# Attention into a gated MLP on one Trainium2 core: the tokens of the first two batches on 96 partitions, and new orders for all engines

## The chip, the cores and the metric

The kernel runs on one core of a Trainium2 chip. The metric is device time in microseconds (us). The core has a matrix engine (TensorE, PE in the profile; its weight loads stand as PEld), a vector engine (VectorE, DVE), an activation engine (ScalarE, ACT), a general engine (GpSimd, POOL) and a queue processor that issues most transfers (SyncE, SP). Transfers run on 16 DMA engines. SBUF is the on-chip memory with 128 partitions, PSUM the accumulator that TensorE writes.

## The reference

There are 8 batches, 8 heads, 576 tokens per head and batch, 64 numbers per token and head, and 32 "pack" queries per head. First the pack queries attend to the tokens, then the tokens attend to the 32 packed results, and the concatenated heads (512 numbers per token, 4608 tokens) go through a two-layer MLP whose activation is h times sigmoid(beta h):

```python
def sm_attn(qq, kk, vv):
    s = scale * np.matmul(qq, kk.transpose(0, 1, 3, 2))
    s = s - np.max(s, axis=-1, keepdims=True)
    a = np.exp(s)
    a = a / (np.sum(a, axis=-1, keepdims=True) + 1e-09)
    return np.matmul(a, vv)
p_packed = sm_attn(p, k, v)
out = sm_attn(q, p_packed, p_packed)
...
h = x @ w_in                                  # 512 -> 2048
g = h * (1.0 / (1.0 + np.exp(-beta * h)))
return (g @ w_out).astype(np.float32)         # 2048 -> 512
```

## The kernel before, in words

**Work of one batch.** k, q and v are loaded in float32 and cast to bfloat16 (`cast`). k and q are transposed, so that the 64 numbers of a head lie on partitions: for batches 0 and 1 on TensorE (`tr`) with copies out of PSUM (`T`), from batch 2 on by transposing DMAs on SP. `s1`, `e1`, `z1`, `i1`, `pun`, `pp` are the first attention (scores, exponentials, sums, inverses, packed values, their copy). `s2`, `e2`, `z2`, `l2`, `n2`, `A2` are the second one, whose normalised weights are `A2`. The packed values are multiplied with w_in ahead of time (`w`, scaled on DVE into `W`), so the first MLP layer is `h` = W times A2, 16 blocks of 128 rows for 512 tokens; ACT applies the activation (`g`). The second layer is `o` (batches 0 and 1, 32 products each, and the leftover tokens) or `p`/`P`, a form with seven products in place of eight (batches 2 to 7).

**Tokens 512 to 575, the rests.** A batch of 576 tokens is cut into 512 main tokens, four on each of 128 partitions, and 64 rest tokens. For k, q and v each rest is loaded by two DMAs of 64 partitions (four heads to partitions 0 to 63, four to 64 to 127; tiles `kr`, `qr`, `vr`), cast on its own, transposed on its own (`trr`), copied on its own (`rk`, `rq`) and has its own scores (`s1r`) and exponentials (`e1r`). In the MLP the rests of two batches share `hr`, `gr` and the product `o` with t = 4, whose two halves are stored by two DMAs (`o_rest`).

**Order.** Nothing schedules at run time. `SEQUENCE` is a table with one list of tasks for each engine, and each engine runs its list in order. `Planner.run` walks through the five lists with a cost in microseconds for each task; with the lists fixed, the costs decide only how the instruction streams are written out and how many keep-warm matmuls (`o_ps<-identr`, result unused) are put into TensorE's gaps before 60 us. SP's list is one queue: a load that waits for its staging buffer holds back all that stand behind it.

**Staging.** w_in and w_out come in four pieces of 1 MB each through three buffers (`stage`). In float32 k, q and v have one buffer of 128 x 2048 each; batches 0 and 1 fill it with two DMAs of 512 KB (four heads each), the later ones with one of 1 MB. Half the first layer of batch 0 can be computed when w_in pieces 0 and 1 are there; its second layer needs all four pieces of w_out, and is cut in two (`HALVED`): `o` 1 to 7 need pieces 0 and 1, `o` 9 to 15 pieces 2 and 3.

**Lines.** All matmuls stand at L382 and all transposes on TensorE at L387, so groups are told apart by tiles. Loads of k, q, v: L434, of rests: L442; of w_in and w_out: L1245 and L1255; casts: L463 (main), L473 (rests), L1251 and L1262 (weights); copies of transposes: L520 and L540; exponentials: L585 and L605; `W`: L795; `A2`: L736; `g`: L827; copy and store of the leftover tokens: L892 and L906.

Of the kernel before, what the change touches and what calls it, by code (L numbers as in the profile page):

```python
# [8 lines left out]
B, H, S, D = 8, 8, 576, 64  # L9
# [12 lines left out]
NC = 4  # L22
# [21 lines left out]
HALVED = (0,)  # L44
TILED = {"w": 1, "s2": 1}
TILED_US = 0.095
# [9 lines left out]
        ("brow", 0), ("tr", 0, "k", 0), ("tr", 0, "k", 1), ("p0_tr", 0), ("p0_tr", 1), ("bcol",), ("brow", 1),  # L56
        ("trr", 0, "k"), ("s1r", 0), ("tr", 0, "q", 0), ("brow", 2), ("s1", 0, 1), ("s1", 0, 0), ("tr", 0, "q", 1),
        ("z1", 0), ("pun", 0, 0), ("pun", 0), ("brow", 3), ("s2", 0, 0), ("z2", 0, 0), ("z2", 0, 1), ("w", 0, 0),
        ("w", 0, 1), ("h", 0, 1), ("h", 0, 2), ("tr", 1, "k", 0), ("h", 0, 0), ("h", 0, 3), ("tr", 1, "k", 1),
        ("o", 0, 0, 1), ("o", 0, 1, 1), ("h", 0, 7), ("h", 0, 4), ("o", 0, 1, 3), ("w", 0, 2), ("trr", 1, "k"),  # L60
        ("o", 0, 0, 3), ("h", 0, 5), ("h", 0, 8), ("s1r", 1), ("trr", 0, "q"), ("h", 0, 6), ("o", 0, 1, 5),
        ("s1", 1, 0), ("o", 0, 0, 5), ("o", 0, 0, 7), ("h", 0, 11), ("s1", 1, 1), ("h", 0, 9), ("o", 0, 1, 7),
        ("o", 0, 2, 1), ("w", 0, 3), ("o", 0, 2, 3), ("o", 0, 3, 1), ("o", 0, 3, 3), ("o", 0, 2, 5), ("z1", 1),
        ("o", 0, 3, 5), ("h", 0, 14), ("o", 0, 2, 7), ("h", 0, 15), ("tr", 1, "q", 0), ("h", 0, 13), ("pun", 1, 0),
        ("h", 0, 12), ("pun", 1), ("tr", 1, "q", 1), ("h", 0, 10), ("o", 0, 3, 7), ("s2", 0, 1), ("s2", 1, 0),
        ("o", 0, 1, 9), ("o", 0, 0, 9), ("w", 1, 0), ("o", 0, 0, 11), ("o", 0, 1, 11), ("z2", 1, 0), ("o", 0, 1, 13),
        ("trr", 1, "q"), ("o", 0, 1, 15), ("z2", 1, 1), ("z2", 0, 2), ("o", 0, 0, 13), ("o", 0, 0, 15),
        ("o", 0, 3, 9), ("o", 0, 3, 11), ("s2", 1, 1), ("w", 1, 1), ("o", 0, 2, 9), ("o", 0, 3, 13), ("z2", 1, 2),
        ("o", 0, 2, 11), ("w", 1, 2), ("o", 0, 2, 13), ("h", 1, 2), ("o", 0, 2, 15), ("h", 1, 1), ("o", 0, 3, 15),
        ("h", 1, 0), ("w", 1, 3), ("h", 1, 5), ("h", 1, 3), ("p_tr", 1), ("h", 1, 4), ("o", 1, 0, 1), ("h", 1, 11),  # L70
        ("p_tr", 0), ("h", 1, 6), ("o", 1, 0, 3), ("h", 1, 8), ("o", 1, 1, 1), ("h", 1, 9), ("h", 1, 10),
        ("o", 1, 1, 3), ("hr", 0, 0), ("h", 1, 7), ("o", 1, 0, 5), ("o", 1, 1, 5), ("s1r", 2), ("hr", 0, 1),
        ("s1", 2, 1), ("o", 1, 0, 7), ("s1", 2, 0), ("h", 1, 15), ("o", 1, 0, 9), ("o", 1, 0, 11), ("o", 1, 1, 7),
        ("z1", 2), ("pun", 2, 0), ("o", 1, 1, 9), ("pun", 2), ("o", 1, 1, 11), ("h", 1, 13), ("h", 1, 12),
        ("w", 2, 0), ("w", 2, 1), ("h", 1, 14), ("o", 1, 1, 13), ("hr", 1, 0), ("o", 1, 0, 13), ("o", 1, 0, 15),
        ("hr", 1, 1), ("o", 1, 1, 15), ("s2", 2, 0), ("w", 2, 2), ("o", 1, 2, 1), ("o", 1, 2, 3), ("z2", 2, 0),
# [274 lines left out]
class Kernel:  # L351
# [57 lines left out]
    def task(self, key, engine, us, fn, deps=(), rank=0, **kw):  # L409
# [4 lines left out]
        return t  # L414


    def plan_loads(self, b):
        nc = self.nc
        rank = 100 * b
        early = b < PE_BATCHES  # L420
        for xi, x in enumerate("kqv" if b == 0 else "kvq"):
            src = self.src[x]
            last = [] if b == 0 else [("cast", b - 1, x, i) for i in range(2)]
            lastr = [] if b == 0 else [("cast", b - 1, x, 2)]
# [919 lines left out]
```

## Time and profile before

| what | us |
|---|---|
| median of 3 runs (246.19 to 246.64) | 246.43 |
| the profiled execution's own time | 246.91 |
| its span, first to last instruction | 245.1 |
| TensorE busy | 231.1 |
| VectorE busy | 148.7 |
| ScalarE busy | 178.8 |
| GpSimd busy | 58.8 |

The profiled execution took 1.8 us more than its span, and 0.5 us more than the median. A busy TensorE includes keep-warm matmuls (132 of them), and waits between dependent matmuls. A row of a stage gives its bounds, then length, the busy time of PE, PEld, DVE, ACT and POOL with the number of instructions, the granted clock of TensorE (1.00 is full), the share of the 16 DMA engines' time that was busy (over 1 when packets overlap), and the rate in GB/s. A row of the timeline gives start, length, engine, line, operation, tiles and shapes, and in brackets the idle time before it and what ended it.

### The profile page before, as it was taken

Reading aid. Unit: us, or ns where it says so; the run is one execution under the profiler, and the core shown is the slowest. Engines: PE = TensorE matmul, PEld = TensorE weight load, DVE = VectorE, ACT = ScalarE, POOL = GpSimd, SP = SyncE. Lnnn points to the kernel's source line nnn. Section 1 sums busy time; section 2 is a strip of 40 time slices with the busy share of each in tenths; the row PEclk is TensorE's granted clock in tenths of the full one; section 3 lists DMA queues with packets and bytes.
Section 4 is the critical chain, followed back from the end, with each engine's and each line's share of the span. In section 5 each row is a group of like instructions: output and inputs, shape, how many; then the busy total and the mean of one; then the engine's idle time right before and its main releaser. Section 6 shows DMA issues by size and latency. Waiting matters only on the chain.

```text
span 245.1 us, 5810 instructions
## 1 busy us (share of the span) xinstructions
PE 231.1 (94%) x2429; PEld 151.0 (62%) x2429; DVE 148.7 (61%) x239; ACT 178.8 (73%) x317; POOL 58.8 (24%) x75
## 2 busy tenths in 40 slices
PE   3997779989999999999999999999999999999992
PEld 3985434633464444787578744886587557667870
DVE  6455566676907937872788376843993368813521
ACT  2486959887797897797779767988798769766210
POOL 4002313206443034207430541061305000000000
PEclk9999999999999999999999999999999999999999
DMA  6999999999989999999999999995993141004024
GB/s 195 298 332 376 305 356 312 366 256 292 199 270 143 277 301 344 183 292 285 280 176 304 325 276 187 337 228 133 195 289 75 36 171 45 1 0 174 0 77 140
DMA packets 74826, 54.13 MB, mean 221 GB/s; under 512 B 42688, under 2 KB 68304, under 8 KB 74800
## 3 DMA queue, kind: packets, MB, share of 16 engines
q1 hardware_dynamic: 74496, 53.68, 85.0%
q8 instruction: 19, 0.31, 0.5%
q10 hardware_dynamic: 304, 0.07, 0.2%
q14 instruction: 7, 0.06, 0.1%
HBM read 37.23 MB, written 9.44 MB: 190 GB/s over the span
## 4 chain that ended last, share of the span: by engine, by line
PE 73%; DMA 16%; issue 5%; POOL 3%; SPq 1%; DVE 0%; POOLq 0%
PE o_ps L382 42%; PE h_ps L382 19%; DMA kr<-in_k_dram 6%; DMA k<-in_k_dram 5%; DMA v<-in_v_dram 5%; PE hr_ps L382 3%; PE w_ps L382 3%; PE s_ps L382 2%; PE z_ps L382 2%; PE pp_ps L382 1%; POOL k_bf L463 1%; POOL p_dup L1172 1%; POOL w_in_bf L1251 1%; SPq L434 0%; PE pT_ps L387 0%
## 5 line engine op out<-in xcount | busy, mean ns | idle before, releaser
L827 ACT ACTIVATE g_main<-h_ps 128x512 bf16<-128x512 f32 x128 | 71.6, 595 | 29.7 <-PE h_ps L382 29.5
L382 PEld LDWEIGHTS <-g_main 128*128 128x128 bf16 x608 | 57.0, 98 | 27.0 <-issue 4.0
L382 PE MATMUL o_ps<-w_out_bf,g_main 128*128 128x256 bf16 (+1 forms) x416 | 72.2, 306 | 0.9 <-ACT w_out_bf L1262 0.5
L382 PE MATMUL h_ps<-A2T,W_bf 128*128 128x512 bf16 x256 | 69.8, 380 | 0.9 <-DVE A2T L736 0.6
L795 DVE SCALAR_TENSOR_TENSOR W_bf<-w_ps,rz,beta_bc 128x512 bf16<-128x512 f32 x64 | 45.1, 745 | 14.5 <-PE w_ps L382 14.4
L382 PEld LDWEIGHTS <-W_bf 128*128 128x128 bf16 x512 | 32.2, 98 | 22.7 <-issue 5.5
L397 ACT ACT_TABLE_LOAD x24 | 30.8, 1283 | 1.1 <-PEq L1328 0.7
L1043 DVE TENSOR_TENSOR o_sb<-o_ps,o_sb 128x512 f32<-128x512 f32 x18 | 12.4, 690 | 24.2 <-PE o_ps L382 21.5
L382 PE MATMUL o_ps<-w_sum,g_main 128*128 128x256 bf16 x192 | 25.9, 273 | 0.0
L382 PE MATMUL o_ps<-w_sum,g_sum 128*128 128x256 bf16 x192 | 24.8, 273 | 0.0
L463 POOL CAST v_bf<-v 128x1024 bf16<-128x1024 f32 x14 | 15.0, 1082 | 37.9 <-DMA v<-in_v_dram 29.0
L382 PEld LDWEIGHTS <-g_sum 128*128 128x128 bf16 x192 | 18.1, 98 | 4.1 <-issue 0.5
L463 POOL CAST q_bf<-q 128x1024 bf16<-128x1024 f32 x12 | 13.2, 1116 | 28.2 <-DMA q<-in_q_dram 14.9
L463 POOL CAST k_bf<-k 128x1024 bf16<-128x1024 f32 x14 | 15.2, 1101 | 16.7 <-DMA k<-in_k_dram 9.7
L382 PE MATMUL o_ps<-w_out_bf,g_rem 128*128 128x512 bf16 x64 | 16.3, 380 | 0.0
L382 PE MATMUL o_ps<-identr 128*128 128x128 bf16 x132 | 11.7, 244 | 3.7 <-DVE bones L1108 3.7
L1045 ACT COPY o_sb<-o_ps 128x512 f32<-128x512 f32 x12 | 7.0, 587 | 10.0 <-PE o_ps L382 10.0
L382 PE MATMUL w_ps<-w_in_bf,pp 64*32 64x512 bf16 x256 | 11.9, 383 | 2.3 <-POOL w_in_bf L1251 1.3
L382 PEld LDWEIGHTS <-identr 128*128 128x128 bf16 x132 | 9.5, 111 | 5.7 <-DVE bones L1108 3.7
L382 PEld LDWEIGHTS <-pp 64*32 64x32 bf16 x384 | 4.3, 89 | 13.5 <-issue 9.3
L695 ACT ACTIVATE E2T<-s_ps,rz 128x512 bf16<-128x512 f32 x16 | 10.7, 688 | 1.8 <-PE s_ps L382 1.3
L736 DVE TENSOR_TENSOR A2T<-E2T,rz 128x512 bf16<-128x512 bf16 x16 | 11.1, 691 | 1.4 <-ACT rz L731 1.4
(99 smaller groups left out, 261.1 us busy)
## 6 DMA issues: line engine op xcount, KB each, us to landing
out_dram<-o_sb SPq DMA_DIRECT2D x14, 512.0 KB, 3.6
k<-in_k_dram SPq DMA_DIRECT2D x6, 1024.0 KB, 8.9
q<-in_q_dram SPq DMA_DIRECT2D x6, 1024.0 KB, 9.1
v<-in_v_dram SPq DMA_DIRECT2D x6, 1024.0 KB, 8.1
w_in<-in_moe_w_in_dram SPq DMA_DIRECT2D x4, 1024.0 KB, 10.3
w_out<-in_moe_w_out_dram SPq DMA_DIRECT2D x4, 1024.0 KB, 10.5
k<-in_k_dram SPq DMA_DIRECT2D x4, 512.0 KB, 9.8
q<-in_q_dram SPq DMA_DIRECT2D x4, 512.0 KB, 7.6
```

What stands on the lines that cost most here:

```text
L382: return self.nc.tensor.matmul(out, lhsT, rhs, start=start, stop=stop, tile_position=pos, skip_group_check=True)
L397: self.nc.scalar.preload_act_table_set(SETS[mode])
L463: self.copy[engine](o[:, 0:2048].rearrange("p (t h d) -> p h t d", t=4, h=8)[:, h], t[:, 0:2048].rearrange("p (h t d) -> p h t d", h=8, t= ...
L695: nc.scalar.activation(st[b, "E2"][:, i, 0:SM], st[b, "s2", i][:], AF.Exp, scale=st[b, "rz1"][:, 2 + i : 3 + i])
L736: nc.vector.tensor_tensor(part(st[b, "A2"], i), part(st[b, "E2"], i), st[b, "rz2"][:, i] if i < 2 else st[b, "rz2r"][:], ALU.mult)
L795: nc.vector.scalar_tensor_tensor(st[b, "W"][:, r, cols], st[b, "w", m][:], st[b, "rz1"][:, r : r + 1], self.beta_bc[:, cols], op0=ALU.mult ...
L827: nc.scalar.activation(st[b, "g"][:, ft, :], st[b, "h", ft][:], AF.Silu)
L1043: nc.vector.tensor_tensor(o, x, o, ALU.add)
L1045: self.copy[engine](o, x)
L1172: self.copy[engine](self.p_dup[0:LATER, :, e, :], self.p32[0:LATER])
L1251: self.copy[engine](self.w_in_bf[:, c, 512 * n : 512 * n + 512], self.t["w_in", n][:, c])
```

## The change

1. **96 partitions.** Batches 0 and 1 put all 576 tokens of a head as six consecutive tokens on each of 96 partitions (`TP, TT = 96, 6`). k, q and v come in two DMAs each of four heads (96 partitions x 4 x 1536 bytes, 576 KB). No rest DMAs, rest casts, rest transposes, `s1r` or `e1r` are left in these batches. Casts are half as long again (1536 numbers on each partition), transposes come in four groups of six for k and for q (one for each pair of heads) with a copy of 576 numbers each, the first attention's scores in three parts in place of two and a rest, its sums in six steps in place of five.
2. **Staging.** The float32 halves go to shared places: the three old buffers and a tile `X` in one of the two buffers of `g`. The second bfloat16 halves of k, q and a part of v go to a tile `Y` in one of the two buffers of `W`. So `w` of batch 1 now waits for the last transposes of batch 1, and `h` of batch 1 for its casts. A batch-1 half waits for the cast of the half before it in its place (`FIRST_SLOTS`).
3. **Zeros.** The fifth block of `E1T` is cleared by POOL after its use in batches 0 and 1 (`ez`), not at the start.
4. **The last product.** In batch 7 the leftover tokens' `o` is computed in two halves of 256 columns (t = 4 and t = 5), each with its own copy and two stores, one on SP's queue and one on ACT's.
5. **Lists.** All five lists of `SEQUENCE` are new. In batch 0 the casts of k move from DVE to ACT, the first cast of v and one of w_in from DVE to POOL. TensorE changes between its plain and its tiled form (`w`, `s2`) 66 times in place of 60, ACT its table 21 times in place of 23, and 111 keep-warm matmuls are left of 132.

```diff
+TP, TT = 96, 6
+FIRST_SLOTS = (
+    {"k": ("k32", "X0"), "q": ("q32", "X1"), "v": ("v32", "k32")},
+    {"k": ("X0", "q32"), "v": ("X1", "v32"), "q": ("k32", "X0")},
+)
...
     "PE": [
-        ("brow", 0), ("tr", 0, "k", 0), ("tr", 0, "k", 1), ("p0_tr", 0), ("p0_tr", 1), ("bcol",), ("brow", 1),
-        ("trr", 0, "k"), ("s1r", 0), ("tr", 0, "q", 0), ("brow", 2), ("s1", 0, 1), ("s1", 0, 0), ("tr", 0, "q", 1),
...
+        ("p0_tr", 0), ("brow", 0), ("bcol",), ("tr", 0, "k", 0), ("tr", 0, "k", 1), ("brow", 1), ("tr", 0, "k", 2),
+        ("tr", 0, "q", 0), ("tr", 0, "k", 3), ("tr", 0, "q", 1), ("brow", 2), ("s1", 0, 0), ("s1", 0, 1),
+        ("tr", 0, "q", 3), ("s1", 0, 2), ("p0_tr", 1), ("tr", 0, "q", 2), ("z1", 0), ("pun", 0, 0), ("pun", 0),
+        ("s2", 0, 0), ("z2", 0, 0), ("w", 0, 0), ("z2", 0, 1), ("brow", 3), ("w", 0, 1), ("h", 0, 3), ("h", 0, 1),
+        ("h", 0, 2), ("h", 0, 0), ("tr", 1, "k", 1), ("tr", 1, "k", 0), ("h", 0, 6), ("h", 0, 5), ("tr", 1, "k", 3),
...
     "SP": [
-        ("ld", 0, "k", 0), ("ld", 0, "k", 1), ("ld", "p0", 1), ("ld", 0, "k", 2), ("ld", 0, "q", 0),
-        ("ld", 0, "v", 0), ("ld", 0, "q", 1), ("ld", 0, "v", 1), ("ld", 0, "v", 2), ("ld_in", 0), ("ld_in", 1),
-        ("ld_out", 0), ("ld", 1, "k", 0), ("ld", 1, "k", 1), ("ld_in", 2), ("ld", 1, "k", 2), ("ld", 0, "q", 2),
-        ("ld_out", 1), ("ld_in", 3), ("ld", 1, "q", 0), ("ld", 1, "v", 0), ("ld", 1, "v", 1), ("ld", 1, "v", 2),
-        ("ld", 1, "q", 1), ("ld_out", 2), ("ld_out", 3), ("ld", 1, "q", 2), ("ld", 2, "k", 0), ("ld", 2, "k", 2),
+        ("ld", 0, "k", 0), ("ld", 0, "k", 1), ("ld", 0, "q", 0), ("ld", 0, "q", 1), ("ld", "p0", 1),
+        ("ld", 0, "v", 0), ("ld", 0, "v", 1), ("ld_in", 0), ("ld_in", 1), ("ld_out", 0), ("ld", 1, "k", 0),
+        ("ld", 1, "k", 1), ("ld_in", 2), ("ld_out", 1), ("ld_in", 3), ("ld", 1, "q", 0), ("ld", 1, "v", 0),
+        ("ld", 1, "q", 1), ("ld", 1, "v", 1), ("ld_out", 2), ("ld_out", 3), ("ld", 2, "k", 0), ("ld", "p"),
...
     "POOL": [
-        ("cast", 0, "k", 2), ("w_in", 0, 0), ("cast", 1, "k", 0), ("cast", 1, "k", 1), ("cast", 1, "k", 2),
+        ("p0_bf", 0), ("cast", 0, "v", 0), ("w_in", 0, 0), ("ez", 0), ("w_in", 1, 0), ("cast", 1, "k", 0),
+        ("w_in", 3, 0), ("cast", 1, "q", 0), ("cast", 1, "v", 0), ("ez", 1), ("p_dup", 0), ("cast", 2, "k", 0),
...
     "DVE": [
+        ("pT", 1), ("i1", 0), ("w_in", 0, 1), ("W", 0, 0), ("w_in", 1, 1), ("A2", 0, 0), ("A2", 0, 1), ("W", 0, 1),
...
+    def plan_first_loads(self, b):
...
+                def load(x=x, i=i, slot=slot):
+                    if slot in ("X0", "X1"):
+                        if "X" not in self.t:
+                            self.t["X"] = self.gp.tile([128, 4096], f32, tag="g", name="x32")
...
+                    nc.sync.dma_start(
+                        t[0:TP, 0:1536].rearrange("p (h e) -> p h e", h=4),
+                        self.src[x][b, 4 * i : 4 * i + 4].rearrange("h (p t) d -> p h (t d)", p=TP),
+                    )
...
+                ld = last = self.task(("ld", b, x, i), "SP", us, load, [self.slot_user.get(slot)], rank + xi)
...
+        def transpose(x, c):
+            st[b, x, "ps", c] = ps = self.att(f"{x}T_ps", bf16)
+            for t in range(TT):
+                self.tp(ps[:, TP * t : TP * t + TP], self.first_block(b, x, c, t), self.identr[0:TP, 0:TP])
...
+        if first:
+            self.task(("ez", b), "POOL", 0.35, lambda: nc.gpsimd.memset(E()[:, 4, :], 0.0), [z1, last], rank + 20)
...
+                n = slice(256 * (t - 4), 256 * (t - 3)) if halves and t >= 4 else slice(0, DM)
...
+            if halves and t >= 4:
+                nc.vector.tensor_copy(st[b, "ob", 2][:, 0, 256 * (t - 4) : 256 * (t - 3)], st[b, "o", t][:, 0:256])
...
+                    queue = nc.scalar if halves and e else nc.sync
+                    queue.dma_start(self.out[lo : lo + SR, n], o[64 * e : 64 * e + 64, 0, n])
```

## The prediction

> **What bounds the kernel now.** I read the page's 40 slices first, then a table of stages, then the timeline where the stages change. The slices (span, engine busy in tenths, DMA share, rate):
>
> ```profile
> span 245.1 us, 5810 instructions
> ...
> PE   3997779989999999999999999999999999999992
> ...
> DMA  6999999999989999999999999995993141004024
> ```
>
> TensorE has gaps only in the first nine slices (up to about 55 us) and in the last; the DMA engines are full for 27 slices. The table of stages (length, then busy time of PE, PEld, DVE, ACT, POOL; the last two numbers are DMA share and GB/s):
>
> ```profile
> 0.00:24.50 24.50, 19.16 (x260) 17.02 (x261) 13.70 (x35) 13.28 (x21) 4.91 (x11) 1.00 0.99 300
> 24.50:58.00 33.50, 29.64 (x271) 14.37 (x269) 22.90 (x41) 28.05 (x52) 8.33 (x9) 1.00 1.10 311
> 58.00:237.00 179.00, 178.59 (x1886) 118.13 (x1884) 110.91 (x163) 136.87 (x245) 45.60 (x56) 1.00 0.81 197
> ```
>
> From 58 us, where the `h` of batch 1 begin, TensorE idles 0.4 us in 179: time falls there only if TensorE gets less work, and it doesn't. Before 24.5 us it mostly waits or runs keep-warm matmuls. Between, it idles 33.5 - 29.64 = 3.9 us, and rows of `o_ps<-identr` (0.55, 0.22, 0.28 and 0.79 us) add 1.8 us of filling. So between the first `h` and those of batch 1 at most 5.7 us can go. What ends the waits there is in the timeline; each of these rows waited for a piece of w_in or w_out:
>
> ```profile
> 31.61 1.30 DVE L1251 CAST w_in_bf<-w_in 128x1024 bf16<-128x1024 f32 x2 [2.34 <-DMA w_in<-in_moe_w_in_dram]
> ...
> 35.57 0.88 DVE L1262 TENSOR_SCALAR w_out_bf<-w_out,rbeta 128x512 bf16<-128x512 f32 x2 [0.73 <-DMA w_out<-in_moe_w_out_dram]
> ```
>
> ```profile
> 51.55 1.33 ACT L1262 ACTIVATE w_out_bf<-w_out,rbeta 128x512 bf16<-128x512 f32 x2 [0.70 <-DMA w_out<-in_moe_w_out_dram]
> ```
>
> So the bound up to 58 us is the order and rate of loads. The rates, by stretches in which one kind of load runs:
>
> ```profile
> 9.00:12.00 3.00, 3.00 (x42) 2.79 (x42) 1.25 (x5) 2.53 (x4) 0.00 (x0) 1.00 1.10 349
> 16.00:20.00 4.00, 3.59 (x53) 2.64 (x49) 1.42 (x5) 2.87 (x5) 0.51 (x1) 1.00 1.05 386
> ...
> 28.00:30.00 2.00, 2.00 (x23) 1.41 (x24) 0.69 (x1) 1.63 (x5) 0.88 (x1) 1.00 1.26 216
> 30.00:32.00 2.00, 2.00 (x10) 0.75 (x8) 0.39 (x1) 1.33 (x3) 0.00 (x0) 1.00 1.09 273
> 32.00:34.00 2.00, 1.11 (x14) 0.53 (x14) 1.76 (x4) 1.13 (x3) 0.73 (x1) 1.00 1.03 361
> ...
> 53.00:57.00 4.00, 4.00 (x37) 1.68 (x34) 3.79 (x8) 3.25 (x10) 0.33 (x1) 1.00 1.08 198
> ```
>
> The first row is main loads of 1 KB pieces on 128 partitions, the second is w_in (2 KB pieces), rows three to five the rests `kr` and `qr` (256-byte pieces on 64 partitions), the last the rests of batch 2 with `p`, the only load before that lies on 96 partitions.
>
> **The change part by part.** I sum against the profiled execution: 246.91 us, 1.8 over its span; the median, 246.43, lies 0.5 lower.
>
> *Loads.* A 512 KB half takes 524 KB / 349 = 1.50 us. The two pairs of rests between 28 and 34 us cost 2 x (169 + 112 + 24) / 385 = 1.58 us of lost rate beside the weights' 385, 0.79 a pair, and 131 KB / 385 = 0.34 for their own bytes: 1.13 a pair. After, a half is 590 KB. On its price the sum hangs. Packets of 1.5 KB lie between the 1 KB and the 2 KB rows, 349 and 386, so 1.61 us at 367. No 128-partition row shows what 96 partitions do; the 96-partition row has 198 GB/s, or 2.98 us. I take 1.69 us, the 1 KB row's rate with no credit for longer pieces: 198 is a mixture with rests, and 128-partition loads beside rests fall as low (216, 273).
>
> Up to the last piece of w_out, before had 12 halves and five pairs of rests ahead: 18.0 + 5.65 = 23.65 us. After: 12 x 1.69 = 20.3, 3.4 us less. On the way: w_in 0 (batch 0 alone, two pairs) 11.26 against 10.14, 1.1 earlier; w_in 2, 0.7 earlier; w_out 1 and w_in 3, where `kr` and `qr` no longer stand ahead, 3.0 earlier, 32.6 and 35.4 us; the last w_out 48.2 in place of 51.5. The batch 2 loads come 4.5 earlier, as a sixth pair goes.
>
> A rule weighs against this. The Trainium skill's SBUF — State Buffer, section "Door 1: The DMA port swizzle", says that partitions 0 to 63 reach only 8 of SBUF's 16 write ports, 64 to 127 the others, at about 27.2 GB/s a port. Two thirds of a 96-partition load would pass through 8 ports: an estimate of 326 GB/s from that page, 1.81 us a half, and 1.4 us less gain than I take (final time 243.5). The row that bears on it is the store of `o_rest`, 64 partitions at a time with nothing beside it: 171 GB/s in 242.3 to 243.8 us, where 128-partition loads of the same 2 KB pieces have 386.
>
> *TensorE up to the first `h`.* The k casts move to ACT (1.04 for 1024 numbers, so 1.5 for 1536, twice) from DVE (0.68). `p0_tr` now stands first on TensorE behind POOL's cast of p (1.0 after its landing at about 7.1), and holds back the transposes of k: 9.8 in place of 9.2 us. `s1` follows at about 13.2, against 12.4 for `s1r` and 13.9 for `s1`. The DVE chain then decides: `W`, a w_in cast, two `A2`, `W` (0.75 + 0.70 + 0.69 + 0.69 + 0.75 = 3.6 us) from about 20.6 puts the first `h` at 24.3; before, one came at 24.55 and the next at 25.57. I count this at nothing (bounds -1.0 and +1.0), since w_out and w_in bind later.
>
> *TensorE from there to 58 us.* The gain there is that of the last w_out, 3.4, and 0.6 more because ACT, whose `l2` and `n2` of batch 1 stood behind two w_out casts (1.33 us), has one of them less there and no `rq` copies (0.36): 4.0 us, below the 5.7 that there are. Cover for the rest: 48 transposes of 96 rows for k and q of a batch cost 46 ns each (`p_dup`: 8 in 0.37) as against 61 (8 in 0.49), so the 96 of both batches cost as the 72 of before; the third part of `s1` and longer `pun` add 0.2 each a batch and stand among TensorE's waits. Casts grow by a third (13824 to 18432 numbers a partition, about 4 us in all), spread on three engines of which the busiest, ACT, has 28.05 of 33.5 us; if that cover is gone, ACT delays `g`, and this half's gain shrinks by up to 2. `ez` (0.31) waits for `pun` with a w_in cast behind it on POOL; `pun` is done by 17, before that w_in lands. SP: the staging waits (`X0`, `k32` and the like) ask for casts that end 5 us or more before the queue gets there, as the full DMA share says that it runs behind.
>
> *After 58 us.* Six more changes of TensorE's form, two of them here, at 0.11 (four `h` take 0.97 after `w`, 0.86 otherwise): +0.2. New order in a stretch that had 0.4 us idle: 0 to 2, I take +0.5.
>
> *The end.*
>
> ```profile
> 237.06 3.62 PE L382 MATMUL o_ps<-w_out_bf,g_rem 128*128 128x512 bf16 x16
> ...
> 240.72 0.69 DVE L892 COPY o_rest<-o_ps 128x512 f32<-128x512 f32 x1 [3.23 <-PE o_ps L382]
> 241.43 1.11 SPq L906 DMA_DIRECT2D out_dram<-o_rest  x2
> ```
>
> 32 products of 256 columns at 109 ns (104 in 11.35 in the chain) take 3.5 us, as 16 of 512 do. The last copy is half as wide: 0.29 (128x256 bf16) to 0.69, I take 0.40, 0.3 less. Then 131 KB in place of 262 go out, on two queues: at 171 to 386 GB/s 0.34 to 0.77 us in place of 1.5, so 0.7 to 1.2 less, I take 0.7. Together -1.0 (-1.5 to -0.2).
>
> Sum: -4.0 - 1.0 + 0.2 + 0.5 = -4.3: 242.6 for the profiled execution, 242.1 for the median.
>
> **The rivals.**
>
> *96-partition loads are slow (slower than before).* The place is every main load of batches 0 and 1. At a half's price t the total moves by 12t - 23.65 - 0.6 - 0.3 us: it turns at t = 2.05 us, 288 GB/s. At 250 GB/s (2.36) it is +3.8, median 250.2; at `p`'s 198 (2.98) +11.2, 257.6. For it: the 198 of the only such load, the 171 of the 64-partition store. Against it: in 53 to 57 us rests of batch 2 run beside `p`.
>
> *Loads come earlier, TensorE doesn't.* ACT, DVE and POOL have more cast work; the first `h` isn't earlier; and the transposed k of batch 2 is issued at 61.11, lands 7.2 later (68.3), and `s1r` of batch 2 uses it at 68.90, so that 0.6 us is all TensorE may gain beyond that transfer. With half of the ramp's gain lost: 244.1; with all but the end, 246.
>
> *The lists' new waits.* Order alone can open waits in 58 to 237 us: each list position differs, and one late `A2` or `W` holds TensorE by its own 0.7. Three to six of these, 2 to 4 us, undo the gain to 244 or 246; with the ramp's gain halved as well, 248.
>
> **How the numbers follow.** Forecast: 0.55, own range 240.6 (rate 367 and the full end) to 243.9 (a half at 320 GB/s, or 1.8 us more of new waits). Part of the gain lost, 243.9 to 245.9: 0.13. Within 0.2% of 246.43 (about what a measurement of this kernel can tell from no change): 0.05. Slow loads: 0.22, of which 0.14 above 250. Slower through waits of the lists: 0.05. Faster 0.68, same 0.05, slower 0.27. The range 240.6 to 250.0 leaves out 0.14 above and 0.04 below.
>
> **What would show it.** Right: 340 GB/s or more while the halves of batch 0 land; w_in's first casts at about 18.4, the last w_out at about 48; first `h` at 24 to 25, `h` of batch 1 at 54; no idle TensorE from there; the span's end within 3.5 us of TensorE's. Wrong: rates near 200 to 290 up to 12 us, w_in past 19.5 and the last w_out past 51.5; waits of `s1r` for the transposed k near 65; idle PE in 58 to 237.

## The result, and the profile after

The changed kernel takes 256.97 us (median of 3 runs, 254.59 to 258.20) against 246.53 us (median of 4, 246.19 to 247.53) for the kernel before on the same chip: 1.0401 times as long, 95% interval 1.0301 to 1.0501. A fourth execution of the changed kernel, 259.32 us, fell in a slower state that some executions of any kernel here show, and this ratio and those below are of the others. A second comparison on another chip gave 1.0351 (1.0273 to 1.0428). Forecast was 242.1 us, at most 250.0. The profiled execution took 254.59 us, the shortest of them, with a span of 252.8, against 246.91 and 245.1 before.

The slices of the page, TensorE, its granted clock and the DMA engines:

```profile
PE   4577989959999999999999999999999999999994
...
PEclk9886899999999999999999999999999999999999
DMA  6999999999999999999999999996793450004115
```

TensorE has thinner slices than before in the second and third (6 to 19 us) and again in the ninth (50 to 57 us). The clock is below full in slices two to five; before, it was full in all. The DMA engines are full for as many slices as before.

The stages, with the bounds of the table shown of before:

```profile
0.00:24.50 24.50, 15.88 (x194) 14.87 (x195) 15.03 (x28) 11.16 (x13) 5.60 (x10) 0.85 0.98 254
24.50:58.00 33.50, 28.98 (x299) 16.85 (x297) 26.11 (x39) 26.36 (x42) 7.13 (x7) 0.95 1.05 303
58.00:237.00 179.00, 178.76 (x1864) 113.57 (x1864) 117.12 (x170) 140.17 (x257) 47.23 (x55) 1.00 0.84 203
```

The last row still has no gap (0.24 us). So the loss lies before it: up to 24.5 us the loads move 254 GB/s in place of 300, and TensorE works 15.88 us in place of 19.16, part of it at half clock.

Shorter stretches of the same table, for the rates:

```profile
9.00:12.00 3.00, 2.58 (x26) 2.30 (x27) 1.23 (x4) 1.42 (x2) 0.36 (x1) 0.75 1.10 242
...
18.00:20.00 2.00, 0.00 (x0) 0.00 (x0) 2.00 (x3) 0.00 (x0) 0.00 (x0) 1.00 1.05 354
20.00:24.00 4.00, 3.77 (x61) 3.54 (x61) 3.70 (x8) 2.66 (x5) 1.09 (x1) 0.59 1.03 382
...
44.00:48.00 4.00, 4.00 (x37) 1.80 (x35) 3.06 (x6) 3.65 (x6) 1.86 (x2) 1.00 1.10 243
```

Halves on 96 partitions run in the first and the fourth row: 242 and 243 GB/s, with the DMA engines fully busy. Weights, on 128 partitions, run in the third: 382. In the second row TensorE does nothing at all while VectorE is busy throughout; in the third its clock is at 0.59.

The timeline at the points that the forecast named (first cast of w_in 0, first `h`, first cast of w_in 2, first casts of the last w_out piece, `h` of batch 1):

```profile
22.77 1.09 POOL L1320 CAST w_in_bf<-w_in 128x1024 bf16<-128x1024 f32 x1 [4.85 <-DMA w_in<-in_moe_w_in_dram]
...
31.22 0.38 PE L389 MATMUL h_ps<-A2T,W_bf 128*128 128x512 bf16 x1
...
36.51 1.04 ACT L1320 CAST w_in_bf<-w_in 128x1024 bf16<-128x1024 f32 x1 [0.48 <-DMA w_in<-in_moe_w_in_dram]
...
59.09 0.94 DVE L1331 TENSOR_SCALAR w_out_bf<-w_out,rbeta 128x512 bf16<-128x512 f32 x2
...
66.20 1.03 PE L389 MATMUL h_ps<-A2T,W_bf 128*128 128x512 bf16 x4
```

Before, the last four stood at 24.55, 31.61, 51.55 and 58.08; the rows of the two `h` were:

```profile
24.55 0.38 PE L382 MATMUL h_ps<-A2T,W_bf 128*128 128x512 bf16 x1
...
58.08 0.60 PE L382 MATMUL h_ps<-A2T,W_bf 128*128 128x512 bf16 x2
```

The last w_out piece itself landed at 57.2 to 57.5 us (issued at 41.5, landed 15.7 to 16.0 later), before at 51.55, when its cast stopped waiting for it. So the loads were about 5.8 us late there; the casts, behind a copy of transposed q on VectorE, were 7.5 late.

For the two profiled executions the sum closes: `h` of batch 1 starts 8.1 us later; from it to TensorE's end it is 182.9 us in place of 182.6, from there to the end of the span 3.7 in place of 4.4; 8.1 + 0.3 - 0.7 = 7.7, the difference of the spans. All that was lost was lost before batch 1's `h`.

What else was new stands in the view of the tile `qT`: first the copies of transposed q out of PSUM, then who waited for them (us, times):

```profile
L564 DVE COPY qT<-qT_ps x6: 2047/2076/2212, 15.3 to 57.3; 128x576 bf16<-128x576 bf16 x6
...
L564 ACT COPY qT<-qT_ps x2: 2083/2091/2099, 23.1 to 56.5; 128x576 bf16<-128x576 bf16 x2
...
  PE pp_ps L389: 2.9, 1
  PE s_ps L389: 2.6, 2
```

The view of the tile `kT` has the copies of transposed k:

```profile
L564 DVE COPY kT<-kT_ps x5: 440/443/452, 14.9 to 38.0; 128x576 bf16<-128x576 bf16 x5
```

A copy of q takes 2.1 us, where copies of transposed k, of as many numbers, take 0.44 on VectorE and 0.64 on ScalarE. The copy of q writes each number 12 bytes from the last. One of the waits, in TensorE's timeline, is the third part of the first attention's scores, which needs a PSUM bank that a copy of q still reads:

```profile
20.23 0.50 PE L389 MATMUL s_ps<-pT,kT 128*96 128x64 bf16 x8 [2.37 <-DVE qT L564]
```

The end, in the timeline:

```profile
245.40 3.66 PE L389 MATMUL o_ps<-w_out_bf,g_rem 128*128 128x256 bf16 x32
...
248.89 1.40 ACTq L970 DMA_DIRECT2D out_dram<-o_rest  x2
249.09 0.42 DVE L950 COPY o_rest<-o_ps 128x256 f32<-128x256 f32 x1 [0.23 <-PE o_ps L389]
```

### The profile page after: what moved, and what is told of

It is laid out like the page before. It is cut to its first block, busy times and chain, and to the rows that moved or that the text cites. A ratio compares the mean times of both kernels' runs of the same rounds, so it can differ in the third digit from the quotient of the medians.

```text
span 252.8 us, 5890 instructions
## 1 busy us (share of the span) xinstructions
PE 235.7 (93%) x2472; PEld 155.9 (62%) x2472; DVE 162.9 (64%) x242; ACT 180.1 (71%) x314; POOL 60.0 (24%) x72
## 4 chain that ended last, share of the span: by engine, by line
PE 80%; DVE 8%; DMA 8%; ACT 1%; SPq 1%; issue 0%; POOL 0%
PE o_ps L389 44%; PE h_ps L389 20%; DMA x<-in_q_dram 5%; DVE qT L564 4%; PE w_ps L389 3%; PE hr_ps L389 3%; DMA p<-in_p_dram 3%; PE s_ps L389 2%; PE z_ps L389 2%; PE pp_ps L389 2%; DVE w_out_bf L1331 1%; PE brow_ps L389 1%; DVE W_bf L851 1%; ACT rz L787 1%; ACT rz L775 0%; PE kT_ps L394 0%
## 5 line engine op out<-in xcount | busy, mean ns | idle before, releaser
L1113 DVE TENSOR_TENSOR o_sb<-o_ps,o_sb 128x512 f32<-128x512 f32 x18 | 12.4, 691 | 25.0 <-PE o_ps L389 20.8
L389 PE MATMUL o_ps<-w_sum,g_sum 128*128 128x256 bf16 x192 | 24.0, 273 | 0.0
L461 POOL CAST q_bf<-q 128x1024 bf16<-128x1024 f32 x12 | 12.6, 1065 | 35.5 <-DMA q<-in_q_dram 31.1
L461 POOL CAST k_bf<-k 128x1024 bf16<-128x1024 f32 x12 | 13.3, 1131 | 16.8 <-DMA k<-in_k_dram 15.3
L389 PE MATMUL o_ps<-w_out_bf,g_rem 128*128 128x512 bf16 (+1 forms) x80 | 16.6, 337 | 0.0
L461 POOL CAST v_bf<-v 128x1024 bf16<-128x1024 f32 x12 | 12.4, 1039 | 17.3 <-DMA v<-in_v_dram 14.6
L792 DVE TENSOR_TENSOR A2T<-E2T,rz 128x512 bf16<-128x512 bf16 x16 | 13.6, 855 | 3.6 <-ACT rz L787 3.5
L611 ACT ACTIVATE E1T<-s_ps 128x512 bf16<-128x512 f32 (+1 forms) x18 | 9.9, 594 | 3.9 <-PE s_ps L389 3.8
L564 DVE COPY qT<-qT_ps 128x576 bf16<-128x576 bf16 x6 | 12.3, 2091 | 0.0
## 6 DMA issues: line engine op xcount, KB each, us to landing
w_in<-in_moe_w_in_dram SPq DMA_DIRECT2D x4, 1024.0 KB, 13.5
```

Of the source, the lines that this page charges most:

```text
L389: return self.nc.tensor.matmul(out, lhsT, rhs, start=start, stop=stop, tile_position=pos, skip_group_check=True)
L461: self.copy[engine](o[:, 0:2048].rearrange("p (t h d) -> p h t d", t=4, h=8)[:, h], t[:, 0:2048].rearrange("p (h t d) -> p h t d", h=8, t= ...
L564: self.copy[engine](o, st[b, x, "ps", c][:, 0:S].rearrange("p (t n) -> p t n", t=TT))
L611: nc.scalar.activation(E()[0:n, 2 * i : 2 * i + 2, :], st[b, "s1", i][0:n].rearrange("p (t e) -> p t e", t=2), AF.Exp, scale=SCALE,)
L792: nc.vector.tensor_tensor(part(st[b, "A2"], i), part(st[b, "E2"], i), st[b, "rz2"][:, i] if i < 2 else st[b, "rz2r"][:], ALU.mult)
L1113: nc.vector.tensor_tensor(o, x, o, ALU.add)
```

## The experiments

Three suspects: the rate of 96-partition loads (240 GB/s, 590 KB in 2.46 us), the copies of q, and TensorE's clock, half in 10.5 to 13.9 and 20.7 to 27.6 us. The lists themselves are a fourth.

### One suspect at a time

*The copies of q, other way round.*

```diff
-            o = o.rearrange("p (t n) -> p t n", t=TT) if x == "k" else o.rearrange("p (n t) -> p t n", t=TT)
-            self.copy[engine](o, st[b, x, "ps", c][:, 0:S].rearrange("p (t n) -> p t n", t=TT))
+            a = st[b, x, "ps", c][:, 0:S]
+            if x == "q":
+                o, a = o.rearrange("p (n t) -> p n t", t=TT), a.rearrange("p (t n) -> p n t", t=TT)
+            self.copy[engine](o, a)
```

> The changed kernel, but the copy that takes transposed q out of PSUM walks its elements the other way round: it writes 576 consecutive numbers and reads with a step of 192 bytes, where it read consecutive numbers and wrote with a step of 12 bytes. Theory (the 12-byte write step is what made these copies 2.1 us instead of the 0.44 and 0.64 that transposed k takes, and they hold TensorE before the first h and in batch 1): the copies fall to 0.4 to 0.9 us, the first h comes 2 to 3 us earlier than 31.2, the whole kernel takes 253 to 255 us instead of 257.6. Rival 1 (any step inside the copy costs the same, on either side): the copies stay above 1.5 us and the time within 0.5 of 257.6. Rival 2 (the loads set the path and the copies lay beside them): the copies fall and the time does not, less than 0.7 us.

Measured: 1.0234 times before (1.0195 to 1.0272). The tile view:

```profile
L566 DVE COPY qT<-qT_ps x6: 735/746/748, 16.8 to 58.0; 128x576 bf16<-128x576 bf16 x6
```

ScalarE's two take 0.64. It is the step in what is written, not a step as such. The time falls by 1.2 to 1.7%, as the theory has it (253.89 us, 253 to 255 expected). The profile shows less: the first `h` comes at 28.3, and the mean granted clock rises from 0.98 to 0.99, but `h` of batch 1 starts at 65.55, only 0.65 earlier than in the changed kernel. The two executions that were profiled took nearly the same time (254.40 us here, a slower one of its kernel; 254.59 there, the fastest of its own). In this pair the copies lie mostly beside waits for loads; how the rest of the gain comes about no profile shows.

*The loads, on 128 partitions.*

```diff
-                        t[0:TP, 0:1536].rearrange("p (h e) -> p h e", h=4),
-                        self.src[x][b, 4 * i : 4 * i + 4].rearrange("h (p t) d -> p h (t d)", p=TP),
+                        t[:, 0:1152].rearrange("p (h e) -> p h e", h=4),
+                        self.src[x][b, 4 * i : 4 * i + 4].rearrange("h s d -> h (s d)").rearrange("h (p e) -> p h e", p=128),
...
-                    t = self.t[b, x, "32", i][0:TP, 0:1536].rearrange("p (h t d) -> p h t d", h=4, t=TT)
+                    t = self.t[b, x, "32", i][0:TP, 0:1152]
+                    t = bass.AP(tensor=t.tensor, offset=t.offset, ap=[list(t.ap[0]), [256, 4], [64, TT], [1, 64]])
```

> The changed kernel with the same bytes of every half of batches 0 and 1 put on 128 partitions (four pieces of 1152 bytes each) instead of on 96 (four of 1536); the casts read as many numbers as before out of the loaded ones, so tokens are in wrong places and the output is not the reference's. Theory (the 96 partitions cost the rate, 240 GB/s where 128 have 350 to 390): the rows of the first 18 us show 330 to 360 GB/s, a half takes 1.65 to 1.8 us, the cast of w_in 0 comes 3 to 4 us earlier than 22.8, and the kernel takes 249 to 252 us. Rival 1 (the rate is low for another reason, the pieces' places in HBM or the waits for staging): 240 to 260 GB/s again, and 256 to 258 us. Rival 2 (loads come earlier, TensorE does not, because the copies of q hold it): rates rise, and the time falls by less than 3 us.

Measured: 1.0131 (1.0093 to 1.0170), 353 to 361 GB/s in 4 to 8 us. First casts of the last w_out piece at 54.3, `h` of batch 1 at 62.2. Better by 2.2 to 2.7% than the changed kernel, and still slower than before, because now the queue of loads stops, as the windows show:

```profile
16.00:20.00 4.00, 2.32 (x28) 2.12 (x27) 4.00 (x4) 1.55 (x3) 1.04 (x1) 0.75 1.03 382
20.00:24.00 4.00, 4.00 (x65) 3.33 (x64) 1.57 (x5) 2.72 (x4) 1.29 (x2) 0.50 1.07 380
24.00:28.00 4.00, 4.00 (x59) 3.14 (x52) 2.15 (x4) 3.80 (x7) 1.46 (x1) 0.90 0.84 301
28.00:32.00 4.00, 3.32 (x34) 1.98 (x32) 4.00 (x8) 3.78 (x7) 0.00 (x0) 1.00 0.74 266
32.00:36.00 4.00, 4.00 (x44) 2.16 (x42) 3.10 (x7) 3.17 (x6) 0.00 (x0) 1.00 0.79 251
```

VectorE is full up to 20 us, three copies of q since 13.3 among its work, so its cast of w_in 0, which clears a buffer, comes at 21.35 (18.22 with short copies); SP issues w_in 2 at 22.12 (18.99 with short copies) and w_out 1 at 27.16 (22.68), and the DMA share falls from 1.06 to 0.84, 0.74 and 0.79: 4 x (0.22 + 0.32 + 0.27) / 1.06 = 3.1 us of transfers not made. TensorE's clock is half here from 18.0 to 24.8 us, behind a wait of 1.8 us for a copy of q. So what slow copies cost beside fast loads includes this half rate; no run has fast loads, slow copies and a full clock.

*Both.* The two diffs together, twice:

> Both edits at once (128 partitions for the halves, consecutive writes of transposed q; output not the reference's for the reason of the first). If the load rate and the copies are the whole of the miss, what was forecast comes: 241 to 245 us, the first h at 24 to 26 us, and the granted clock at full rate in the first 25 us. If the order of the new lists or the clock gate is a cause by itself, it stays at 247 or more, with the clock still at half rate in part of the first 25 us or with waits in 25 to 58 us that end neither on a load nor on a copy of q.

> The kernel with both edits once more, for an undisturbed profile: 241 to 244 us, first h at 24 to 26 us, granted clock 0.99 to 1.00, TensorE's busy time in 0 to 58 us as before or higher.

Measured: 0.9781 times before (0.9745 to 0.9817), and 242.26 us in the second execution, whose profile has these stages and moments:

```profile
0.00:24.50 24.50, 20.39 (x277) 17.79 (x277) 13.87 (x33) 15.45 (x24) 7.47 (x12) 1.00 0.98 328
24.50:58.00 33.50, 32.79 (x311) 16.87 (x311) 29.38 (x52) 29.34 (x52) 11.12 (x10) 1.00 1.08 339
```

```profile
24.19 0.38 PE L389 MATMUL h_ps<-A2T,W_bf 128*128 128x512 bf16 x1
...
29.38 1.04 ACT L1323 CAST w_in_bf<-w_in 128x1024 bf16<-128x1024 f32 x1 [0.36 <-DMA w_in<-in_moe_w_in_dram]
...
46.46 0.88 DVE L1334 TENSOR_SCALAR w_out_bf<-w_out,rbeta 128x512 bf16<-128x512 f32 x2 [0.20 <-DMA w_out<-in_moe_w_out_dram]
...
53.40 1.03 PE L389 MATMUL h_ps<-A2T,W_bf 128*128 128x512 bf16 x4
```

The forecast had 24.3 for the first `h`, 48.2 for the last w_out, which came 1.7 earlier, and 54 for `h` of batch 1. With these two causes gone, the total of the sum holds, lists included, and the clock is full by itself. The two cures give 1.2 to 1.7% (copies) and 2.2 to 2.7% (loads) alone and 5.7 to 6.2% together: while one cause is there, part of the other hides behind it.

*The clock alone.* The planner's costs put right, so that 95 more keep-warm matmuls stand in TensorE's gaps:

```diff
-                us = 1.63 if b or not i else 1.8
+                us = 2.46
...
-                    ("T", b, x, c), {"DVE": 0.4, "ACT": 0.6}, None, lambda e, x=x, c=c: evacuate(x, c, e),
+                    ("T", b, x, c), {"DVE": 0.44, "ACT": 0.64} if x == "k" else {"DVE": 2.1, "ACT": 2.1}, None, lambda e, x=x, c=c: evacuate(x, c, e),
```

> The changed kernel with the planner's costs put right (2.46 us a half in place of 1.63, 2.1 us a copy of transposed q in place of 0.4 and 0.6). The lists fix the order, so only the keep-warm matmuls change: 95 more of them stand in front of TensorE's waits. Theory (the clock gate is a cause of its own: of the 11 us lost some come from half rate between 10 and 28 us): the granted clock stays at full rate there, its mean rises from 0.97 to 0.99 or more, and the time falls by 1 to 3 us, to 254.5 to 256.5. Rival (the half-rate stretches lie beside waits for loads and copies that end when they end): the clock is full and the time moves by less than 0.7 us. Rival 2 (the more matmuls stand in the way of real work): slower by up to 1 us.

Measured: 1.0299 (1.0250 to 1.0347). The clock's row of the page has no dent left:

```profile
PEclk9999999999999999999999999999999999999999
```

With the copies short as well:

> The changed kernel with consecutive writes of transposed q and with the planner's costs put right (2.46 us a half, 0.75 and 0.64 us a copy of q), so that only the slow loads are left: lists, loads and computation as in the changed kernel. The forecast's own sum, with a half at 2.46 us (12 x 2.46 - 23.65 - 0.9 = +5.0), gives 2.0% over the kernel before. Either cure alone gave 2.3% (copies) and 3.0% (costs). Theory (both cures take away the same thing, half rate of TensorE's clock; the copies lay beside waits for loads): 1.9 to 2.4% over before. Rival (the copies cost time of their own on the path, over the clock): 1.0 to 1.7%.

Measured: 1.0278 (1.0204 to 1.0351), above the 1.9 to 2.4% expected, though the interval reaches into it. The clock was not full all the time in the profile: it is half from 32.8 to 36.1 us. And the changed kernel once more:

> The changed kernel as it is on the same chip and in the same hour, since the comparisons between its variants go through the kernel before on other chips: 1.030 to 1.050 times before, granted clock between 0.96 and 0.98 and differing from execution to execution, times spread over 3 us or more where the variants with a full clock spread over 1 to 2.

Measured: 1.0351 (1.0273 to 1.0428), clock 0.966 to 0.980, spread 3.1 us. The four kernels with slow loads thus stand at 1.023 to 1.040; what the copies and the clock add to slow loads is 0.5 to 1.7%, and these intervals overlap too much to divide it between the two. In the changed kernel a lower clock does go with a longer time (0.980 with 254.59 to 255.98 us, 0.966 with 258.05 and 258.20); with short copies no such order shows (0.984 with 252.28, 0.993 with 254.40).

### The price of a load by itself

Transfers, and copies, behind the last store of the kernel before:

```diff
+            t = self.in32.tile([128, 2048], f32, tag=x + "32", name=name)
+            engine.dma_start(
+                t[lo : lo + P, 0 : c * e].rearrange("p (c e) -> p c e", c=c),
+                flat[off : off + P * c * e].rearrange("(c p e) -> p c e", c=c, p=P),
+            )
...
+        for lo, P, c, e in SETS_APART:
+            for x in "kqv":
+                off = rows(f"m{P}at{lo}x{4 * e}", x, nc.sync, lo, P, c, e, off)
```

> The kernel before, with transfers and copies appended behind its last store that nothing uses, so that each is measured by itself; the time of the whole grows by all of them and says nothing. Transfers, three of each form, from q: 128 partitions x 4 pieces of 2048, 1536 and 1152 bytes; 96 partitions (0 to 95) x 4 of 1536 and x 3 of 2048; 96 partitions from 16 to 111; 112 partitions; 64 partitions from 0 and from 32; and 48 + 48 partitions (0 to 47, 64 to 111) on two queues. Theory A (the halves of the partitions, 0 to 63 and 64 to 127, have separate ways in, and 96 from 0 load one of them twice as much): 240 to 260 GB/s for 0 to 95 whatever the piece, 330 to 390 for 16 to 111, and 64 from 32 about twice 64 from 0 (200 and up to 390). Theory B (fewer partitions, fewer GB/s, wherever they lie): 16 to 111 as slow as 0 to 95, 64 from 32 as slow as 64 from 0. Theory C (the piece of 1536 bytes is slow): 128 partitions of 1536 at 240 to 260 as well, and 96 of 2048 faster. Copies of 576 numbers with a step of 1, 2, 3, 6 and 9 numbers in what is written, and of 6 in what is read, on VectorE from PSUM and from SBUF and on ScalarE from PSUM: theory, 0.44 us (VectorE) and 0.64 (ScalarE) for step 1, and above 1.5 us from some step on that is at most 6; a step of 6 in what is read 0.75 and 0.65. Rival: the time grows evenly with the step.

The windows: 128 partitions of 2048 and of 1536 bytes, 96 partitions (0 to 95) of 1536 bytes, 16 to 111, 0 to 95 of 2048 bytes, 112 partitions, 64 from 0 and 64 from 32 (left out: 128 of 1152 bytes at 357, the two queues at 206):

```profile
246.00:252.00 6.00, 0.00 (x0) 0.00 (x0) 5.86 (x5) 0.00 (x0) 0.00 (x0) 0.53 1.03 389
254.50:259.00 4.50, 0.00 (x0) 0.00 (x0) 4.34 (x4) 0.00 (x0) 0.00 (x0) 0.50 1.07 374
261.00:266.00 5.00, 0.00 (x0) 0.00 (x0) 0.00 (x0) 0.00 (x0) 0.00 (x0) 0.50 1.09 238
268.00:273.50 5.50, 0.00 (x0) 0.00 (x0) 0.00 (x0) 0.00 (x0) 0.00 (x0) 0.50 1.09 238
276.00:281.00 5.00, 0.00 (x0) 0.00 (x0) 0.00 (x0) 0.00 (x0) 0.00 (x0) 0.50 1.07 248
...
289.00:295.00 6.00, 0.00 (x0) 0.00 (x0) 0.00 (x0) 0.00 (x0) 0.00 (x0) 0.50 1.09 232
297.00:303.00 6.00, 0.00 (x0) 0.00 (x0) 0.00 (x0) 0.00 (x0) 0.00 (x0) 0.50 1.05 202
304.50:308.00 3.50, 0.00 (x0) 0.00 (x0) 0.00 (x0) 0.00 (x0) 0.00 (x0) 0.50 1.04 322
```

Theory C falls: 1536-byte pieces have 374 on 128 partitions, and 2048-byte pieces 248 on 96. Theory A falls as well: 96 partitions laid evenly over the halves have the same 238, and even 112 have 232. Theory B falls with 64 from 32, at 322 against 202 from 0, though it had 16 to 111 right. The copies, from VectorE's timeline (PSUM to SBUF, with a step of 1, 6 and 9 numbers in what is written, then of 6 in what is read; steps of 2 and 3, left out, take 0.80 and 1.11):

```profile
244.39 0.40 DVE L1342 COPY P_w<-c_ps 128x576 bf16<-128x576 bf16 x1
...
248.82 2.07 DVE L1342 COPY P_w<-c_ps 128x576 bf16<-128x576 bf16 x1
...
252.07 2.68 DVE L1342 COPY P_w<-c_ps 128x576 bf16<-128x576 bf16 x1
...
257.51 0.76 DVE L1342 COPY P_r<-c_ps 128x576 bf16<-128x576 bf16 x1
```

Out of PSUM the time grows with the step of the writes, nearly evenly, as the rival has it; the theory's limit of 1.5 us is passed between 3 and 6. ScalarE has 0.64 to 2.68 for the same five write steps. Out of SBUF VectorE takes 0.31, 0.49, 1.11, 1.12 and 2.69, where a step of 6 costs no more than one of 3.

Why 96 and 112 are slow was asked once more:

> The kernel before with transfers appended behind its last store, three of each form, nothing else to do. Open is why 96 and 112 partitions run at 240 GB/s wherever they start, while 64 from 32 has 322 and 64 from 0 has 202. Theory S (each of 16 DMA engines takes a sixteenth of the partitions, neighbours; four neighbouring partitions from a multiple of 4 share a way into SBUF, and so do partitions 32 apart in the same half; an engine has full rate only where no other writes the same way): 64 partitions from 34 fall to 215 to 240 though they lie as evenly over the halves as those from 32; 64 from 16 about 205; 64 with a step of 2 (0, 2, ... 126) and 32 with a step of 4 about 205; 96 from 32 about 210 to 250. Theory H (only the balance of the halves 0 to 63 and 64 to 127 counts): 34 and both stepped forms as fast as from 32 (310 to 390), 64 from 16 about 270. 128 partitions of 3 x 2304 bytes: 390 or more by both, the price of a layout that puts two heads of 64 groups of nine tokens on 128 partitions: 590 KB in 1.5 us.

Windows for 128 partitions of 2304 bytes, 64 from 34, 64 from 16, and 64 with a step of 2 (64 from 32: 316; 96 from 32: 236; 32 with a step of 4: 203, from transfers too short to fill the engines, DMA share 0.70):

```profile
244.50:250.00 5.50, 0.00 (x0) 0.00 (x0) 0.00 (x0) 0.00 (x0) 0.00 (x0) 0.52 1.04 393
...
257.00:261.50 4.50, 0.00 (x0) 0.00 (x0) 0.00 (x0) 0.00 (x0) 0.00 (x0) 0.50 1.04 264
263.00:268.50 5.50, 0.00 (x0) 0.00 (x0) 0.00 (x0) 0.00 (x0) 0.00 (x0) 0.50 1.06 208
270.00:274.50 4.50, 0.00 (x0) 0.00 (x0) 0.00 (x0) 0.00 (x0) 0.00 (x0) 0.50 0.95 274
```

Theory H is out: a shift by two partitions, with the halves nearly as even, brings 316 down to 264, and 64 from 16 have 208 where H had 270. Theory S had 64 from 16 and 96 from 32 right, but its figures for 34 (215 to 240) and for the step of 2 (205) are too low. So the position of the partitions matters, by as little as two; a rule that gives 96 partitions their 240 stays open.

The Trainium skill's DMA: Bandwidth & Descriptors, section "The descriptor swizzle", has each of the 16 engines write a port of its own in a 128-partition transfer; the 357 to 393 GB/s of all 128-partition forms do not contradict that, and what it means for 96 no run here shows.

### Other ways to load

*Wide.* All 128 partitions with six tokens each, a third of the partitions' bytes unread:

```diff
+                    a = self.src[x][b, 4 * i : 4 * i + 4]
...
+                        t[:, 0:1536].rearrange("p (h e) -> p h e", h=4),
+                        bass.AP(tensor=a.tensor, offset=a.offset, ap=[[TT * D, 128], [S * D, 4], [1, TT * D]]),
```

> A version that computes the reference: the changed kernel with consecutive writes of transposed q, and each half loaded on all 128 partitions with six tokens each. Partitions 0 to 95 hold what they held; 96 to 127 receive the 192 tokens that follow in memory and nobody reads them, so a half moves 786 KB instead of 590. The planner's cost of a half is set to 2.1 us, which changes only the number of keep-warm matmuls. Measured apart, 128 partitions of 1536-byte pieces ran at 375 GB/s and 96 at 240: a half takes 786 / 375 = 2.10 us instead of 2.46. If the price of a half sets the time (254 us at 2.46, 242.8 at 1.65 with the same copies), 2.10 gives 0.4% over the kernel before, 247.9 to 249.5 us where before has 247.5. Rival: the extra bytes keep the loads at 2.4 us or more, 252 us and up.

Measured: 1.0017 (0.9982 to 1.0052); 302 to 391 GB/s in 4 to 16 us, first casts of the last w_out piece at 53.1. Moving a third more bytes is 2% faster than leaving 32 partitions out (1.0234 with the same copies).

*Split.* Partitions 32 to 95, then 0 to 31, in two transfers:

```diff
+                    a = self.src[x][b, 4 * i : 4 * i + 4].rearrange("h (p t) d -> p h (t d)", p=TP)
+                    for r in (slice(32, 96), slice(0, 32)):
+                        nc.sync.dma_start(t[r, 0:1536].rearrange("p (h e) -> p h e", h=4), a[r])
```

> As the one before, but each half in two transfers without extra bytes: partitions 32 to 95 first (apart: 322 GB/s and 88 ns a packet of 2 KB, against 202 GB/s and 168 ns for 64 partitions from 0), then 0 to 31. By those rates a half takes 393 KB / 322 + 197 KB / 202 = 2.2 us one after the other, 1.9 to 2.0 where the two overlap. By the same line through 254 (2.46) and 242.8 (1.65): 246.5 to 249.5 us, so -0.4% to +0.8% against before. Rival: two issues a half and shorter transfers give it back, 252 us and up.

Measured: 1.0175 (1.0112 to 1.0239), a miss, in the rival's range: 207 to 267 GB/s in 4 to 16 us, so a half takes some 2.4 us, more than the 2.2 that the two rates apart (322 and 202) give one after the other. Why the better form gains nothing here no run shows.

*Stacked.* Two heads on 128 partitions, nine tokens each, and 64 x 64 squares on TensorE:

```diff
+                        t[:, 0:1152].rearrange("p (c e) -> p c e", c=2),
+                        self.src[x][b, 4 * i : 4 * i + 4].rearrange("h s d -> (h s d)").rearrange("(c p e) -> p c e", c=2, p=128),
...
+                for r in range(2):
+                    h, a = slice(64 * r, 64 * r + 64), S * c + 64 * t
+                    self.tp(ps[h, 64 * t : 64 * t + 64], st[b, x][h, a : a + 64], self.identr[h, h], (64 * r, 64 * r))
```

> A version that computes the reference: the changed kernel's lists with another layout of batches 0 and 1: two neighbouring heads lie side by side on 128 partitions, 64 groups of nine tokens each, so that a half is 2 pieces of 2304 bytes on 128 partitions; transposes, scores and packing then work on 64 x 64 squares of TensorE, one for each head (18 transposes for a column block instead of 6, 24 products a score task instead of 8, 36 a packing task instead of 12; about 375 more short products in all), and q is written in consecutive numbers. Theory (the price of a half sets the time, and TensorE has room up to 58 us): a half at 590 KB / 390 = 1.51 us, 12 x 1.51 - 23.65 - 0.9 = -6.4: 239.5 to 243 us, faster than both kernels. Rival (the added products fill TensorE: 192 transposes at 31 ns or more and 192 products at 20 to 45 ns are 10 to 15 us, half of it in 24 to 58 us, where 5.7 us were free): the loads are early, TensorE is dense from 24 us on, and the time is 245 to 252 us.

Measured: 1.0298 (1.0259 to 1.0338), 254.86 us. The loads do what was wanted (349 to 389 GB/s up to 24 us), but neither the theory nor the rival's dense TensorE comes. Two rows of TensorE's timeline, and the windows behind them:

```profile
15.92 0.44 PE L394 MATMUL qT_ps<-identr,q_bf 64*64 64x64 bf16 x17 [1.62 <-issue]
...
22.11 1.28 PE L389 MATMUL pp_ps<-E1T,v_bf 64*64 64x32 bf16 x32 [1.17 <-issue]
```

```profile
16.00:24.00 8.00, 6.83 (x167) 6.40 (x167) 2.58 (x6) 2.73 (x7) 2.09 (x3) 0.56 1.05 388
24.00:28.00 4.00, 4.00 (x40) 2.41 (x38) 0.54 (x1) 2.37 (x5) 1.90 (x2) 0.60 0.62 225
```

TensorE stops twice for something the profile does not name, runs at half clock from 17 to 27 us, and the first `h` comes at 30.4; the weights' buffers are cleared late again, and the DMA share falls to 0.62, then 0.44. The early loads were worth nothing here, where the chain to the first `h` got longer.

### The end alone

The kernel before, with only the last rest in halves:

```diff
+                n = slice(256 * (t - 4), 256 * (t - 3)) if halves and t >= 4 else slice(0, DM)
...
+                    queue = nc.scalar if halves and e else nc.sync
```

> The kernel before with one part of the change alone: the last rest of batch 7 as two halves of 256 columns, each with a copy of its own, and its stores on two queues. Forecast in the document: -1.0 us (-0.2 to -1.5). In the changed kernel the stretch from TensorE's end to the end of the span went from 4.4 to 3.7 us, so -0.7: 245.6 to 246.0 us. Rival (more products and a store issue on ACT give it back): within 0.3 us of 246.5.

> The kernel before with the halved last rest alone, for a narrower interval: ratio 0.997 (0.995 to 0.998), about -0.7 us, as its profile and the first comparison gave. Rival: nothing measurable, 0.999 to 1.001.

Measured: 0.9971 (0.9942 to 1.0000) and 0.9955 (0.9916 to 0.9994): -0.7 and -1.1 us; the first interval just reaches no change. Of the versions that compute all of the reference it is the only one below both kernels.

## Why the prediction was wrong

**The price of a half** failed: "I take 1.69 us", from a row of 128 partitions, because the 198 GB/s of `p` was read as a mixture with rests. The rests explain at most the last of it: any 96 partitions have 236 to 248 with nothing beside them. A half so takes 2.46 us, and the signs that the forecast had named for being wrong came (242 GB/s in 9 to 12 us, w_in at 22.8, the last w_out at 59.1). At 2.46 us the forecast's own sum, 12t - 23.65 - 0.6 - 0.3, gives +5.0 us, 2.0%; 1.023 to 1.030 was measured with slow loads and the clock or the copies cured. Its part for the loads alone, 12t - 23.65, gives +5.9 us for the last w_out, which landed 5.8 later. At the 2.10 and 1.65 us of the wide and the 128-partition loads the whole sum gives +0.3 and -1.9%; 0.2 and -2.2 were measured. So the sum holds to about a percent, with its turning point (2.05 us, 288 GB/s), and one term carried 9.2 of some 15 us of miss. The rest goes with the copies and the clock, but for 0.3 to 1.0% that is not accounted for. The rival that ended slower was this one; its own figure at 198 GB/s, 257.6, lies near the measured time by luck, since loads at 240 alone give 251.4. The range was cut at 2.36 us although the row nearest in form bounded it at 2.98.

**The copies of transposes** failed by omission. The paragraph on cover counted transposes and casts, and no copy of q. Eight copies of 2.1 us replace four of 0.7 to 1.0 and smaller ones of the rests (0.36); VectorE is busy 162.9 us in place of 148.7. Six lie on VectorE, which also makes `W`, `A2` and the casts that clear the weights' buffers. With fast loads they cost 3.5% (1.0131 against 0.9781, half rate of the clock included), with loads on 96 partitions 1.7% at most.

**The clock** was in no step. TensorE's idle stretches of 2.5 and 2.4 us (for POOL's cast of p, which landed late, and for a copy of q) were followed by half rate for 3.4 and 6.8 us; with both causes gone there was none, so it came with the other two and was not a cause of its own. The length of a wait does not tell by itself: in the same execution 2.9 us of idling before 53.0 us was followed by no half rate, and in the kernel with short copies none followed 3.3 us before 10.2, but 3.4 us of half rate followed 1.7 us before 52.5.

The Trainium skill's TensorE: Matmul & The Clock Gate, Part 1: The HAM clock gate, has half rate after an idle window of about 3.4 us and full rate after as long a busy one; 3.4 and 6.8 us are one and two such windows, though the wait before each was shorter.

**SP's staging waits** were called harmless. In the changed kernel that nearly held: the DMA share falls below 0.95 only in 36 to 40 us, to 0.88. With fast loads and slow copies it did not: the weights' three buffers, which the forecast did not look at, held the queue.

**The chain to the first `h`**, counted at nothing with bounds of 1.0, ended 6.9 later than its 24.3. Once loads and copies were as assumed, its end was right (24.19), in part by luck, since steps on the way were later than forecast: the transposes of k at 10.1 (11.0 in the changed kernel), not 9.8, because `brow` and `bcol` stand between them and `p0_tr` in the list, and `s1` at 14.3, not 13.2.

**Right** were: TensorE dense from 58 to 237 us; the stretch behind `h` of batch 1, +0.3 (+0.7 forecast); the end, -0.7 (-1.0), with copies of 0.42 (0.40); and the order of the moments of w_in and w_out, each 0.2 to 1.7 us earlier with both cures than forecast.

The rule weighed against the change, the Trainium skill's SBUF — State Buffer, section "Door 1: The DMA port swizzle", pointed the right way and not far enough: the estimate from it was 326 GB/s, 240 was measured, and the measurement decides. It does not by itself tell the cases apart, since 96 partitions from 16, even over both halves, have 238. The page's port formula has 8 ports for 64 partitions from 0, all 16 from 32 and 12 from 16. At its 27.2 GB/s a port that makes estimates of 218, 435 and 326 GB/s, where 202, 316 to 322 and 208 were measured: the first agrees, the others do not.

## What to carry to other kernels

A load is priced by a row of its own form, partition count included; where the only such row is a bad one (198 on 96 partitions here), that row belongs in the range and the form is worth one transfer measured apart before a layout is built on it. When a layout moves, price every instruction that touches it by the step of its writes as well as by the count of its numbers: 576 two-byte numbers out of PSUM cost VectorE 0.40 to 2.68 us by step alone, and reading with a step of 6 instead of writing with it costs 0.76 in place of 2.07. And two causes that hide behind each other must be removed together before either is judged small.

## What the runs showed of the hardware

- Loads into SBUF, measured apart: 357 to 393 GB/s on 128 partitions (1152 to 2304-byte pieces), 236 to 248 on 96 from 0, 16 or 32, 232 on 112, and on 64 from 0, 16, 34 and 32 202, 208, 264 and 316 to 322. Two 48-partition transfers on two queues have 206.
- Copies of 576 2-byte numbers out of PSUM slow down with the step of the writes, and by nearly the same amounts on VectorE and ScalarE from a step of 6 bytes on (1.11, 2.1, 2.68 us for steps of 3, 6, 9 numbers). Out of SBUF, VectorE takes 1.12 for a step of 6.
- TensorE's half rate lasts 3.4 us or about two or three times that (10.5 to 13.9 and 20.7 to 27.6 us in the changed kernel, 18.0 to 24.8 with fast loads, 52.8 to 56.1 with short copies, 17.0 to 27.2 in the stacked one). It came behind waits of 1.6 to 2.5 us, and other waits, up to 3.3 us, passed without it.
- In the stacked kernel, with some 375 more short products, TensorE has stops of 1.62 and 1.17 us that end on nothing in the profile. The trace has a 16 KB packet on the queue for instructions at 13.5 to 14.6 and at 19.7 to 20.8 us, and TensorE resumed 1.3 us after each; that it waited for its code is argued from that, not shown.
